# Decode attention over a large KV cache: V in one SBUF buffer and K in two, where K and V shared three in turn

## The chip, the cores and the metric

The kernel runs on one core of one Trainium2 chip. The metric is the device time of one execution in microseconds; shorter is better. Engines are named as the profile names them: PE (TensorE, matrix products; PEld is its weight load), DVE (VectorE), ACT (ScalarE), POOL (GpSimd) and SP (SyncE, which here only issues DMAs).

## What is computed

Two independent blocks A and B, with the same shapes, each compute one decode step of attention. Cut to what matters:

```python
# x (2, 1, 640), k and v (2, 32, 8192, 192), wq (640, 6144), wo (6144, 640), all bfloat16
q = (x @ wq).reshape(B, Sq, H, Dh).transpose(0, 2, 1, 3)
scores = jnp.einsum("bhqd,bhkd->bhqk", q, k_cache) * (Dh ** -0.5)
p = jax.nn.softmax(scores, axis=-1)
o = jnp.einsum("bhqk,bhkd->bhqd", p, v_cache)
y = o.transpose(0, 2, 1, 3).reshape(B, Sq, H * Dh) @ wo
```

The output is the two results side by side. With one query per head, each element of K and V is used once; the two caches of both blocks make up most of the bytes.

## The kernel before, in words

**Units.** The work is cut into 64 units. A unit `u` is two heads of one batch row of one block; its K is 128 partitions x 128 positions x 192 channels (6 MB, 48 KB in each partition), with the two heads in partitions 0-63 and 64-127, and its V has the same form. For a unit:

- `m(u,c)`, c = 0..3: DVE multiplies a quarter of K by the query (`dve_mul`, L285) into one of two product buffers, `prod[c % 2]`.
- `s(u,c)`: PE adds up the product over the channels by 12 matmuls with an identity (`pe_sum`, L362) into a PSUM tile of `scps`; `r(u,c)`: DVE sums the last 16 channels (`dve_red`, L289) into the scores `sc`.
- `mx(u)`: DVE takes the maximum (`dve_max`, L295); `ar(u)`: POOL takes it over the partitions (`pool_ar`, L266); `nb(u)` and `exp(u)`: ACT negates it (L315) and computes the exponentials `pb` and their sums `rs` (`act_exp`, L324).
- `l(u)` and `pv(u)`: PE sums `rs` over the partitions (L368) and multiplies by V in 64 matmuls (`pe_pv`, L376) into `ops`.
- `rc`, `oh`, `os` (DVE, L300 to L306) and `of` (ACT, L309): the division, the result into `qall`.

Before the units, `x` and the two `wq` are loaded and the queries of all heads computed (`pe_q`, L354); after them come a transpose (`pe_turn`, L390) and the product with `wo` (`pe_out`, L404), whose weights are loaded in pieces into buffers that have come free.

**Buffers.** `big` holds three buffers `kv` of a unit's K or V (48 KB of each partition) and the two product buffers. The list `loads` (L209) is k0, k1, v0, k2, v1, ..., k63, v62, v63, and load `i` goes into buffer `i % 3` (L216). All loads are issued by SP in that order on one DMA queue. Load `i` waits for whoever used load `i-3` (`done`, L480): the last product `m(u,3)` for a K, `pv(u)` for a V. The smaller tiles (`sc`, `mp`, `mg`, `nb`, `rs`, `pb`, `rc`, `ops`) and `scps` have three copies each.

**Order of the work.** Each engine's instructions are put into a table by slot and order number (`put`, L418) and emitted in that order; semaphore waits come from the keys. In a slot `u` the order is

- DVE: m(u,0), m(u,1), r(u,0), m(u,2), r(u,1), m(u,3), r(u,2), r(u,3), mx(u), then rc, oh, os of unit u-2;
- PE: s(u,0), s(u,1), s(u,2), s(u,3), l(u-1), pv(u-1);
- ACT: nb(u), exp(u), of(u-2).

DVE, ACT and PE run most units in hardware loops of three units; SP and POOL are straight code.

Of the kernel before, what the change touches and what calls it, by code (L numbers as in the profile page):

```python
# [12 lines left out]
class _Stream:  # L13
    virtual = set()

    def __init__(self, name, sem, reg, first=3):
# [101 lines left out]
def build_kernel(nc, blocks, out):  # L118
# [28 lines left out]
    with ExitStack() as es:  # L147
# [4 lines left out]
        rc = [sb(f"rc{i}", [2, 1], F32) for i in range(3)]  # L152
# [4 lines left out]
        pb = [sb(f"pb{i}", [128, 2 * T], BF16) for i in range(3)]  # L157
        actd = sb("actd", [128, 2], F32)
        xw = sb("xw", [128, NBLK * DC * 128 + D], BF16)
        sc = [sb(f"sc{i}", [128, T], F32) for i in range(3)]  # L160
        mp = [sb(f"mp{i}", [128, 2], F32) for i in range(3)]
        mg = [sb(f"mg{i}", [128, 2], F32) for i in range(3)]
        nb = [sb(f"nb{i}", [128, 1], F32) for i in range(3)]
        rs = [sb(f"rs{i}", [128, 2], F32) for i in range(3)]
# [7 lines left out]
        ops = [ps(f"ops{i}", [128, 512], F32) for i in range(3)]  # L172
        scps = [ps(f"scps{i}", [128, TC, DG], F32) for i in range(3)]
# [3 lines left out]
        oacc = [outps[:], qbank[(LASTU * NCH + 1) % 3]]  # L177
        qps = qbank + [outps[:]]
# [16 lines left out]
        S_pe = _Stream("pe", sem("s_pe"), reg, 1)  # L195
# [16 lines left out]
        loads += [("v", LASTU)]  # L212
        buf = {}
# [6 lines left out]
        bk, b62, b63 = buf["k", LASTU], buf["v", LASTU - 1], buf["v", LASTU]  # L220
        assert (bk, b62, b63) == (2, 0, 1)
        woA, wo0, wo1 = bk * BUFE, b62 * BUFE, b63 * BUFE
        pieces = []
        for blk, rows, off, w in ((0, (WR,), woA, [("s", LASTU, NCH - 1)]), (1, (29,), wo0, [("pv", LASTU - 1)]),
                                  (1, (11, 5, 2, 1), wo1, [("pv", LASTU)])):
            r = 29 if off == wo1 else 0
            for n in rows:
                pieces.append((blk, r, r + n, off, w))
                off, r, w = off + n * D, r + n, []
            assert r == (29 if off == wo0 + 29 * D else WR)  # L230
        NA = 0
        assert 29 * D <= BUFE and woA + WR * D <= NBUF * BUFE + 2 * PRODE
# [21 lines left out]
        def ld_wo(n):  # L254
            blk, r0, r1, off, _ = pieces[n]
            src = blocks[blk]["wo"].rearrange("(p i) n -> p (i n)", i=WR)
            return dma(big[:, off:off + (r1 - r0) * D], src[:, r0 * D:r1 * D], ("wo", n))

        def ld_kv(kind, u):
            hp, b = u // B, u % B  # L260
            blk, h = hp // PPB, 2 * (hp % PPB)
            src = blocks[blk][kind][b, h:h + 2].rearrange("s (p t) d -> (s p) t d", p=64)
            return dma(kv[buf[kind, u]], src, (kind, u))

        def pool_ar(u):
            return lambda eng: eng.partition_all_reduce(mg[u % 3][:], mp[u % 3][:], 128, bass.bass_isa.ReduceOp.max)  # L266
# [21 lines left out]
        def dve_red(u, c):  # L288
            return lambda eng: eng.tensor_reduce(sc[u % 3][:, c * TC:(c + 1) * TC], scps[(u * NCH + c) % 3][:], AXL.X, ALU.add)  # L289

        def dve_max(u):
            def fn(eng):
                for s in range(2):
                    r = slice(64 * s, 64 * s + 64)
                    ins = eng.tensor_reduce(mp[u % 3][r, s:s + 1], sc[u % 3][r, :], AXL.X, ALU.max)  # L295
                return ins
            return fn

        def dve_rc(u):
            return lambda eng: eng.reciprocal(rc[u % 3][:], ops[u % 3][0:2, QW:QW + 1])  # L300

        def dve_ohi(u):
            return lambda eng: eng.tensor_copy(o_hi[:], ops[u % 3][32:34, Dh:QW])  # L303

        def dve_osum(u):
            return lambda eng: eng.tensor_tensor(o_sum[:], ops[u % 3][0:2, 0:Dh], o_hi[:], ALU.add)  # L306

        def act_of(u):
            return lambda eng: eng.activation(qall[0:2, S_act.at(u), :], o_sum[:].unsqueeze(1), ACTF.Identity, scale=rc[u % 3][:])  # L309

        def act_nb(u):
            def fn(eng):
                for s in range(2):
                    r = slice(64 * s, 64 * s + 64)
                    ins = eng.activation(nb[u % 3][r, :], mg[u % 3][r, s:s + 1], ACTF.Identity, scale=-scale)  # L315
# [3 lines left out]
        def act_exp(u):  # L319
            def fn(eng):  # L320
                for s in range(2):
                    r = slice(64 * s, 64 * s + 64)
                    dst = pb[u % 3][r, :].rearrange("p (g a j s) -> p g a j s", a=2, j=JB, s=2)[:, :, :, :, s]
                    ins = eng.activation(dst, sc[u % 3][r, :].rearrange("p (g j a) -> p g a j", j=JB, a=2),  # L324
                                         ACTF.Exp, bias=nb[u % 3][r, :], scale=scale, accum_out=rs[u % 3][r, s:s + 1])
# [33 lines left out]
        def pe_sum(u, c):  # L359
            def fn(eng):  # L360
                for j in range(NJ):
                    ins = eng.matmul(scps[(u * NCH + c) % 3][:], ident[:], prod[c % 2][:, :, j * DG:(j + 1) * DG],  # L362
# [4 lines left out]
        def pe_l(u):  # L367
            return lambda eng: eng.matmul(ops[u % 3][0:2, QW:QW + 1], rs[u % 3][:], ones[:], start=True, stop=True)  # L368

        def pe_pv(u):  # L370
            vv = kv[buf["v", u]].rearrange("p (j a) d -> p j (a d)", a=2)

            def fn(eng):
                for j in range(TJ):
                    j0s = 4 * JB * (j // JB) + 2 * (j % JB)
                    ins = eng.matmul(ops[u % 3][0:MP, 0:QW], pb[u % 3][:, j0s:j0s + MP], vv[:, j, :],  # L376
# [20 lines left out]
        def pe_out(n):  # L397
            blk, r0, r1, off, _ = pieces[n]
            wo = big[:, off:off + (r1 - r0) * D].rearrange("p (i n) -> p i n", n=D)
# [9 lines left out]

        def pe_idle(eng):  # L410
            for i in range(8):
                ins = eng.matmul(ops[(LASTU + 1) % 3][:], ident[:], big[:, woA + 512 * i:woA + 512 * (i + 1)], start=True, stop=True)
            return ins
# [21 lines left out]
        for u in range(NU):  # L435
            for c in range(NCH):
                w = [("k", u), ("pq", NP - 1), ("qa", NP - 1), ("qx", NP - 1), back("s", u, c, 2)]
                slot, order = (0, 9.2) if (u, c) == (1, 0) else (u, 2 + 2 * c)
                put("dve", slot, order, dve_mul(u, c), w, ("m", u, c), ("m", c, u % 3))
                put("dve", u, 5 + 2 * c if c < NCH - 1 else 9.5, dve_red(u, c),  # L440
                    [("s", u, c), key("mx", u - 3), key("exp", u - 3)], ("r", u, c), ("r", c, u % 3))
                put("pe", u, 0.1 * c, pe_sum(u, c),
                    [("m", u, c), ("os", -2) if (u, c) == (1, 0) else None, back("r", u, c, 3), ("id1",), ("qx", NP - 1), ("qa", NP - 1)], ("s", u, c), ("s", c, u % 3))
            put("dve", u, 12, dve_max(u), [("r", u, NCH - 1), key("ar", u - 3), ("init",)], ("mx", u), ("mx", u % 3))
            put("pool", u, 0, pool_ar(u), [("mx", u), key("nb", u - 3)], ("ar", u), ("ar", u % 3))
            put("act", u, 0, act_nb(u), [("ar", u), key("exp", u - 3)], ("nb", u), ("nb", u % 3))
            put("act", u, 1, act_exp(u), [("nb", u), key("pv", u - 3), key("l", u - 3), ("init",)], ("exp", u), ("exp", u % 3))
            w0 = [("exp", u), key("os", u - 3), key("rc", u - 3), ("init",)]
            pslot = u + 1
            pe_o = 2  # L450
            put("pe", pslot, pe_o, pe_l(u), w0, ("l", u), ("l", u % 3))
            put("pe", pslot, pe_o + 0.1, pe_pv(u), [("v", u)], ("pv", u), ("pv", u % 3, buf["v", u]))
            put("dve", u + 2, 20, dve_rc(u), [("pv", u), key("of", u - 3)], ("rc", u), ("rc", u % 3))
            put("dve", u + 2, 21, dve_ohi(u), [("pv", u), key("os", u - 1)], ("oh", u), ("oh", u % 3))
            put("dve", u + 2, 22, dve_osum(u), [("oh", u), key("of", u - 1)], ("os", u), ("os", u % 3))
            put("act", u + 2, 4, act_of(u), [("os", u), ("rc", u)], ("of", u), ("of", u % 3))
# [11 lines left out]
        put("act", NU, 6, act_ot(0), [("t", 1, HQ - 1)], ("ot", 0))  # L468
        put("act", E2, 6, act_ot(1), [("t", 1, HL)], ("ot", 1))
        for n, p in enumerate(pieces):  # L470
# [3 lines left out]
            put("pe", E2, 0.01 * n if n <= NA else 2 + 0.01 * n, pe_out(n), w, ("f", n))  # L474
        put("pe", E2, 1, pe_idle, [("of", LASTU)], None)
# [3 lines left out]

        def done(i):  # L480
            if i < 0:
                return None
            kind, u = loads[i]
            return ("m", u, NCH - 1) if kind == "k" else ("pv", u)
# [10 lines left out]
        for n in range(len(pieces)):  # L495
# [11 lines left out]
        fills = [(mp[i], -3.0e38) for i in range(3)] + [(t[i], 0.0) for i in range(3) for t in (rs, pb)]  # L507
        for n, (t, v) in enumerate(fills):
            S_pool.add((lambda t, v: (lambda eng: eng.memset(t[:], v)))(t, v), sig=("init",) if n == len(fills) - 1 else None)
        for n in range(128 // HP):  # L510
# [10 lines left out]
                              ("r", u, 2), ("r", u, 3), ("mx", u), ("rc", u - 2), ("oh", u - 2), ("os", u - 2)],  # L521
            "act": lambda u: [("nb", u), ("exp", u), ("of", u - 2)],
# [89 lines left out]
```

## Time and profile before

| | |
|---|---|
| median of 3 runs | 1937.36 us (1937.12 to 1937.49) |
| span of the profiled execution | 1936.0 us, 1.4 us under that median (no other time of that execution is given) |
| PE, DVE, ACT, POOL busy | 80%, 58%, 7%, 1% of the span |
| mean granted TensorE clock | 0.929 of full speed |
| moved by DMA | 836.91 MB, mean 432 GB/s |

A share of busy time is an average over the span. The chain of waits follows the work that ended last back from its end. In a timeline row the columns are start and length in us, engine, line, operation, output <- inputs, and in brackets the idle time ahead and who ended it; `SPq` rows are DMA issues. "us to landing" counts from a DMA's issue to its last byte's report.

### The profile page before, as it was taken

The page shows a single profiled execution, that of the slowest core. Times are in us where ns is not written, and L with a number is a line of the kernel's source. Part 1 is how long each engine was busy: PE and PEld are TensorE (multiplying, and loading weights), DVE is VectorE, ACT ScalarE, POOL GpSimd, SP SyncE. Part 2 cuts the span into 40 slices and gives each one's busy share as a digit, 9 for nine tenths or more (in the row PEclk, how much of TensorE's full clock was granted, in tenths as well). Part 3 has the DMA queues.
Part 4 walks back from the last instruction along what each step waited for, and adds up shares of the span by engine and source line. Part 5 has one row for each costly group of instructions (what it writes and reads, how often), then busy time and mean ns, then how long its engine had stood idle before and what let it go on. Part 6 is the DMA issues. An engine that isn't in the chain of part 4 may idle for free.

```text
span 1936.0 us, 19059 instructions
## 1 busy us (share of the span) xinstructions
PE 1545.0 (80%) x7728; PEld 743.0 (38%) x7729; DVE 1124.0 (58%) x907; ACT 142.3 (7%) x519; POOL 28.4 (1%) x113
## 2 busy tenths in 40 slices
PE   5777878878878878878878878878878878878878
PEld 2333434434434434434434434433433433433434
DVE  4765565565565565565565565565565565565560
ACT  3100000000000000000000000000000000000000
POOL 0000000000000000000000000000000000000000
PEclk9899989988989988989988999999999999999999
DMA  9999999999999999999999999999999999999999
GB/s 419 427 435 436 432 434 438 430 434 437 434 433 434 437 431 435 437 432 433 436 436 431 434 438 429 436 437 432 434 435 436 430 436 438 428 436 437 433 433 391
DMA packets 19610, 836.91 MB, mean 432 GB/s; under 512 B 2184, under 2 KB 2320, under 8 KB 2576
## 3 DMA queue, kind: packets, MB, share of 16 engines
q1 hardware_dynamic: 19600, 836.78, 99.9%
q8 instruction: 6, 0.10, 0.0%
q14 instruction: 4, 0.03, 0.0%
HBM read 836.77 MB, written 0.01 MB: 432 GB/s over the span
## 4 chain that ended last, share of the span: by engine, by line
DMA 49%; PE 31%; DVE 17%; issue 3%; DVEq 0%; SPq 0%; ACT 0%; ACTq 0%
DMA big<-in_B_k_cache_dram 24%; DMA big<-in_A_k_cache_dram 22%; PE ops L376 18%; DVE big L285 15%; PE scps L362 12%; DMA big<-in_B_wq_dram 2%; DVE sc L289 1%; DMA big<-in_B_wo_dram 1%; PE scps L354 0%; PE ops L368 0%; PE outps L354 0%; DVEq L285 0%; DVE qall L275 0%; PE scps L404 0%; PE oTps L390 0%
## 5 line engine op out<-in xcount | busy, mean ns | idle before, releaser
L285 DVE TENSOR_TENSOR big<-big,qall 128x6144 bf16<-128x6144 bf16 x256 | 852.7, 3351 | 490.7 <-DMA big<-in_B_k_cache_dram 260.6
L362 PE MATMUL scps<-big,ident 128*128 128x512 bf16 x3072 | 815.6, 426 | 358.2 <-DVE big L285 355.7
L376 PE MATMUL ops<-big,pb 128*34 128x384 bf16 x4096 | 676.8, 326 | 0.0
L362 PEld LDWEIGHTS scps<-big,ident 128*128 128x128 bf16 x3072 | 314.3, 107 | 852.7 <-DVE big L285 439.2
L376 PEld LDWEIGHTS ops<-big,pb 128*34 128x34 bf16 x4096 | 395.5, 98 | 258.7
L289 DVE TENSOR_REDUCE sc<-scps 128x32 f32<-128x512 f32 x256 | 175.9, 687 | 227.7 <-PE scps L362 227.7
L315 ACT ACTIVATE nb<-mg 64x1 f32<-64x1 f32 x128 | 25.8, 201 | 1707.7 <-POOL mg L266 1706.9
L324 ACT ACTIVATE pb<-sc,nb 64x128 bf16<-64x128 f32 x128 | 55.8, 436 | 7.8
L266 POOL PARTITION_ALL_REDUCE mg<-mp x64 | 25.7, 402 | 1859.1 <-DVE mp L295 1859.1
L295 DVE TENSOR_REDUCE mp<-sc 64x1 f32<-64x128 f32 x128 | 35.9, 280 | 8.3
L309 ACT ACTIVATE qall<-o_sum,rc 2x192 f32 (+1 forms) x64 | 29.0, 453 | 20.7 <-DVE o_sum L306 19.1
L306 DVE TENSOR_TENSOR o_sum<-ops,o_hi 2x192 f32<-2x192 f32 x64 | 22.1, 346 | 7.7
L354 PE MATMUL scps<-big,xw 128*128 x120 | 23.2, 351 | 2.6 <-DVE xw L271 2.2
L324 ACT ACTIVATION_READ_ACCUMULATOR pb<-sc,nb 64x1 f32 x128 | 23.7, 185 | 0.0
L303 DVE COPY o_hi<-ops 2x192 f32<-2x192 f32 x64 | 22.3, 349 | 2.0
L300 DVE RECIPROCAL rc<-ops 2x1 f32<-2x1 f32 x64 | 10.0, 156 | 21.3 <-PE ops L376 19.3
L275 DVE CAST qall<-scps 64x192 f32 x48 | 17.0, 355 | 7.2 <-PE scps L354 5.4
L280 ACT ACTIVATE qall<-scps 64x192 f32 x48 | 15.6, 324 | 30.5 <-DVE qall L275 28.2
L345 PE MATMUL oTps<-ident,xw 4*128 4x4 bf16 x5 | 0.4, 178 | 21.5 <-DMA xw<-in_B_x_dram 21.5
L354 PEld LDWEIGHTS scps<-big,xw 128*128 128x128 bf16 x120 | 12.4, 103 | 12.1 <-issue 5.9
L368 PEld LDWEIGHTS ops<-ones,rs 128*2 128x2 f32 x128 | 5.5, 82 | 26.9 <-issue 26.9
L404 PE MATMUL outps<-big,oT 128*2 128x320 bf16 x96 | 9.2, 369 | 4.6 <-DMA big<-in_A_wo_dram 4.6
(36 smaller groups left out, 67.6 us busy)
## 6 DMA issues: line engine op xcount, KB each, us to landing
big<-in_A_k_cache_dram SPq DMA_DIRECT2D x32, 6144.0 KB, 28.6
big<-in_A_v_cache_dram SPq DMA_DIRECT2D x32, 6144.0 KB, 27.6
big<-in_B_k_cache_dram SPq DMA_DIRECT2D x32, 6144.0 KB, 28.9
big<-in_B_v_cache_dram SPq DMA_DIRECT2D x32, 6144.0 KB, 27.8
big<-in_A_wq_dram SPq DMA_DIRECT2D x1, 7680.0 KB, 21.2
big<-in_B_wq_dram SPq DMA_DIRECT2D x1, 7680.0 KB, 38.2
big<-in_A_wo_dram SPq DMA_DIRECT2D x1, 7680.0 KB, 29.0
big<-in_B_wo_dram SPq DMA_DIRECT2D x1, 4640.0 KB, 29.3
```

The source lines that it names most:

```text
L266: return lambda eng: eng.partition_all_reduce(mg[u % 3][:], mp[u % 3][:], 128, bass.bass_isa.ReduceOp.max)
L285: return lambda eng: eng.tensor_tensor(prod[c % 2], t[:, c * TC:(c + 1) * TC, :], qall[:, S_dve.at(u), :].broadcast_to([128, TC, Dh]), ALU ...
L289: return lambda eng: eng.tensor_reduce(sc[u % 3][:, c * TC:(c + 1) * TC], scps[(u * NCH + c) % 3][:], AXL.X, ALU.add)
L295: ins = eng.tensor_reduce(mp[u % 3][r, s:s + 1], sc[u % 3][r, :], AXL.X, ALU.max)
L303: return lambda eng: eng.tensor_copy(o_hi[:], ops[u % 3][32:34, Dh:QW])
L306: return lambda eng: eng.tensor_tensor(o_sum[:], ops[u % 3][0:2, 0:Dh], o_hi[:], ALU.add)
L309: return lambda eng: eng.activation(qall[0:2, S_act.at(u), :], o_sum[:].unsqueeze(1), ACTF.Identity, scale=rc[u % 3][:])
L315: ins = eng.activation(nb[u % 3][r, :], mg[u % 3][r, s:s + 1], ACTF.Identity, scale=-scale)
L324: ins = eng.activation(dst, sc[u % 3][r, :].rearrange("p (g j a) -> p g a j", j=JB, a=2), ACTF.Exp, bias=nb[u % 3][r, :], scale=scale, acc ...
L354: ins = eng.matmul(qps[hp % NQ][:, 0:QW], xbc[:, blk, c, :], wq_t[blk][:, c, S_pe.at(off, QW, QW)], start=(c == 0), stop=(c == DC - 1))
L362: ins = eng.matmul(scps[(u * NCH + c) % 3][:], ident[:], prod[c % 2][:, :, j * DG:(j + 1) * DG], start=(j == 0), stop=(j == NJ - 1))
L376: ins = eng.matmul(ops[u % 3][0:MP, 0:QW], pb[u % 3][:, j0s:j0s + MP], vv[:, j, :], start=(j == 0), stop=(j == TJ - 1))
```

## The change

- **Buffers.** V always has buffer 2; K of unit u has buffer `u % 2`. So the load of k(u) waits for m(u-2,3), and that of v(u) for pv(u-1). The order of the loads on SP stays, up to the last ones.
- **Order on PE:** s(u,0), s(u,1), s(u,2), l(u-1), pv(u-1), s(u,3): the V product stands ahead of the fourth quarter's sums.
- **Order on DVE:** m(u,1), r(u,0), m(u,2), r(u,1), m(u,3), r(u,2), rc, oh, os of u-1, then m(u+1,0) of the next unit, then r(u,3), mx(u).
- **Order on ACT:** of(u-1), nb(u), exp(u).
- **Tiles.** The small tiles have one copy each instead of three, `scps` has four copies (one a quarter), the query phase uses these four.
- **Loops** of one unit on PE and ACT, of two on DVE and (new) on SP; POOL stays straight code.
- **Tail.** 38 of the 48 rows of A's `wo` (rows of 128 x 640) are loaded into K's buffer 0 after m(62,3), ahead of v(63); 10 rows of A and 28 of B follow into the K buffers after s(63,3), 19 rows of B into the product buffers and one into `xw`. No piece of `wo` waits for pv(63) now. The 8 matmuls of `pe_idle` (L410) are gone, and A's first 38 rows are multiplied ahead of pv(63).

```diff
-        for i, (kind, u) in enumerate(loads):
-            buf[kind, u] = i % NBUF
-            bcount[i % NBUF] += 1
-            reg[(kind, u)] = (bsem[i % NBUF], 16 * bcount[i % NBUF])
+            n = VB if kind == "v" else u % VB
+            buf[kind, u] = n
+            bcount[n] += 1
+            reg[(kind, u)] = (bsem[n], 16 * bcount[n])
...
-                slot, order = (0, 9.2) if (u, c) == (1, 0) else (u, 2 + 2 * c)
-                put("dve", slot, order, dve_mul(u, c), w, ("m", u, c), ("m", c, u % 3))
+                put("dve", u if c else u - 1, 2 + 2 * c if c else 9.3, dve_mul(u, c), w, ("m", u, c), ("m", c, u % VB))
                 put("dve", u, 5 + 2 * c if c < NCH - 1 else 9.5, dve_red(u, c),
-                    [("s", u, c), key("mx", u - 3), key("exp", u - 3)], ("r", u, c), ("r", c, u % 3))
-                put("pe", u, 0.1 * c, pe_sum(u, c),
+                    [("s", u, c), key("exp", u - 1)], ("r", u, c), ("r", c))
+                put("pe", u, 0.1 * c if c < NCH - 1 else 3, pe_sum(u, c),
...
-            put("dve", u + 2, 20, dve_rc(u), [("pv", u), key("of", u - 3)], ("rc", u), ("rc", u % 3))
+            put("dve", u + 1, 9.20, dve_rc(u), [("pv", u), key("of", u - 1)], ("rc", u), ("rc",))
...
-        for i, (kind, u) in enumerate(loads):
-            w = [done(i - NBUF)]
-            if i in (1, 2):
-                w = [("pq", PPB * i - 1)]
-            S_sp.add(ld_kv(kind, u), waits=w)
+        for kind, u in loads[:-1]:
+            if kind == "k":
+                load(kind, u, [("pq", PPB - 1)] if u == 1 else [key("m", u - VB, NCH - 1)] if u else [])
+            else:
+                load(kind, u, [key("pv", u - 1)] if u else [("pq", NP - 1)])
+        S_sp.add(ld_wo(0), waits=pieces[0][4])
+        load("v", LASTU, [("pv", LASTU - 1)])
+        for n in range(1, len(pieces)):
             S_sp.add(ld_wo(n), waits=pieces[n][4])
...
-                S_dve.emit(eng, [(PQ0, PQ0 + NP, NQ), (3, NSLOT, 3)])
+                S_dve.emit(eng, [(PQ0, PQ0 + NP, NQ), (1, NSLOT, VB)])
...
-                S_pe.emit(eng, [(PQ0, PQ0 + PPB, NQ), (PQ0 + PPB, PQ0 + NP, NQ), (1, NSLOT, 3)])
+                S_pe.emit(eng, [(PQ0, PQ0 + PPB, NQ), (PQ0 + PPB, PQ0 + NP, NQ), (1, NSLOT, 1)])
```

`VB` is 2, `NCH` 4, `LASTU` 63.

More of the change, by code (lines that the diff above doesn't have):

```diff
@@ L14, with __init__ @@
     virtual = set()
-    def __init__(self, name, sem, reg, first=3):
+    def __init__(self, name, sem, reg, first=1):
         self.first = first
@@ L150, in build_kernel @@
         sem = lambda name: es.enter_context(nc.semaphore(name))
-        rc = [sb(f"rc{i}", [2, 1], F32) for i in range(3)]
+        rc = sb("rc", [2, 1], F32)
+        nb = sb("nb", [128, 1], F32)
+        rs = sb("rs", [128, 2], F32)
         o_hi = sb("o_hi", [2, Dh], F32)
@@ L156, in build_kernel @@
         qall = sb("qall", [128, NU, Dh], BF16)
-        pb = [sb(f"pb{i}", [128, 2 * T], BF16) for i in range(3)]
+        pb = sb("pb", [128, 2 * T], BF16)
         actd = sb("actd", [128, 2], F32)
         xw = sb("xw", [128, NBLK * DC * 128 + D], BF16)
[L160 to L164, printed above, removed]
+        sc = sb("sc", [128, T], F32)
+        mp = sb("mp", [128, 2], F32)
+        mg = sb("mg", [128, 2], F32)
         ident = sb("ident", [128, 128], BF16)
@@ L170, in build_kernel @@
         out_sb = sb("out_sb", [HP + B, D], BF16)
-        ops = [ps(f"ops{i}", [128, 512], F32) for i in range(3)]
-        scps = [ps(f"scps{i}", [128, TC, DG], F32) for i in range(3)]
+        ops = ps("ops", [128, 512], F32)
+        scps = [ps(f"scps{i}", [128, TC, DG], F32) for i in range(NCH)]
         outps = ps("outps", [128, 512], F32)
@@ L215, in build_kernel @@
         for i, (kind, u) in enumerate(loads):
-            buf[kind, u] = i % NBUF
-            bcount[i % NBUF] += 1
-            reg[(kind, u)] = (bsem[i % NBUF], 16 * bcount[i % NBUF])
-        bk, b62, b63 = buf["k", LASTU], buf["v", LASTU - 1], buf["v", LASTU]
-        assert (bk, b62, b63) == (2, 0, 1)
-        woA, wo0, wo1 = bk * BUFE, b62 * BUFE, b63 * BUFE
+            n = VB if kind == "v" else u % VB
+            buf[kind, u] = n
+            bcount[n] += 1
+            reg[(kind, u)] = (bsem[n], 16 * bcount[n])
+        FREE0, FREE1 = [("m", LASTU - 1, NCH - 1)], [("m", LASTU, NCH - 1), ("s", LASTU, NCH - 1)]
+        BIG, XW = 0, 1
+        PROD = NBUF * BUFE
         pieces = []
-        for blk, rows, off, w in ((0, (WR,), woA, [("s", LASTU, NCH - 1)]), (1, (29,), wo0, [("pv", LASTU - 1)]),
-                                  (1, (11, 5, 2, 1), wo1, [("pv", LASTU)])):
-            r = 29 if off == wo1 else 0
+        for blk, rows, t, off, w in ((0, (38, 10), BIG, 0, FREE0), (1, (28,), BIG, WR * D, FREE1),
+                                     (1, (12, 5, 2), BIG, PROD, []), (1, (1,), XW, 0, [])):
             for n in rows:
[L228 to L232, printed above, removed]
+                r = sum(p[2] - p[1] for p in pieces if p[0] == blk)
+                pieces.append((blk, r, r + n, (t, off), w))
+                off, w = off + n * D, FREE1 if t == BIG and off == 0 else []
+        assert sum(p[2] - p[1] for p in pieces) == NBLK * WR
+        assert 76 * D <= VB * BUFE and 19 * D <= 2 * PRODE
+        NA = 1
         for n in range(len(pieces)):
@@ L288, in dve_red @@
         def dve_red(u, c):
-            return lambda eng: eng.tensor_reduce(sc[u % 3][:, c * TC:(c + 1) * TC], scps[(u * NCH + c) % 3][:], AXL.X, ALU.add)
+            return lambda eng: eng.tensor_reduce(sc[:, c * TC:(c + 1) * TC], scps[c][:], AXL.X, ALU.add)
         def dve_max(u):
@@ L299, in dve_rc @@
         def dve_rc(u):
-            return lambda eng: eng.reciprocal(rc[u % 3][:], ops[u % 3][0:2, QW:QW + 1])
+            return lambda eng: eng.reciprocal(rc[:], ops[0:2, QW:QW + 1])
         def dve_ohi(u):
-            return lambda eng: eng.tensor_copy(o_hi[:], ops[u % 3][32:34, Dh:QW])
+            return lambda eng: eng.tensor_copy(o_hi[:], ops[32:34, Dh:QW])
         def dve_osum(u):
-            return lambda eng: eng.tensor_tensor(o_sum[:], ops[u % 3][0:2, 0:Dh], o_hi[:], ALU.add)
+            return lambda eng: eng.tensor_tensor(o_sum[:], ops[0:2, 0:Dh], o_hi[:], ALU.add)
         def act_of(u):
-            return lambda eng: eng.activation(qall[0:2, S_act.at(u), :], o_sum[:].unsqueeze(1), ACTF.Identity, scale=rc[u % 3][:])
+            return lambda eng: eng.activation(qall[0:2, S_act.at(u), :], o_sum[:].unsqueeze(1), ACTF.Identity, scale=rc[:])
         def act_nb(u):
@@ L361, in fn @@
                 for j in range(NJ):
-                    ins = eng.matmul(scps[(u * NCH + c) % 3][:], ident[:], prod[c % 2][:, :, j * DG:(j + 1) * DG],
+                    ins = eng.matmul(scps[c][:], ident[:], prod[c % 2][:, :, j * DG:(j + 1) * DG],
                                      start=(j == 0), stop=(j == NJ - 1))
@@ L367, in pe_l @@
         def pe_l(u):
-            return lambda eng: eng.matmul(ops[u % 3][0:2, QW:QW + 1], rs[u % 3][:], ones[:], start=True, stop=True)
+            return lambda eng: eng.matmul(ops[0:2, QW:QW + 1], rs[:], ones[:], start=True, stop=True)
         def pe_pv(u):
@@ L375, in fn @@
                     j0s = 4 * JB * (j // JB) + 2 * (j % JB)
[L376 removed]
+                    ins = eng.matmul(ops[0:MP, 0:QW], pb[:, j0s:j0s + MP], vv[:, j, :],
                                      start=(j == 0), stop=(j == TJ - 1))
@@ L397, in pe_out @@
         def pe_out(n):
-            blk, r0, r1, off, _ = pieces[n]
-            wo = big[:, off:off + (r1 - r0) * D].rearrange("p (i n) -> p i n", n=D)
+            blk, r0, r1, (t, off), _ = pieces[n]
+            wo = (big, xw)[t][:, off:off + (r1 - r0) * D].rearrange("p (i n) -> p i n", n=D)
             def fn(eng):
@@ L408, in pe_out @@
             return fn
[L410 to L413, printed above, removed]
         NSLOT = NU + 8
@@ L447, in build_kernel @@
-            put("act", u, 1, act_exp(u), [("nb", u), key("pv", u - 3), key("l", u - 3), ("init",)], ("exp", u), ("exp", u % 3))
-            w0 = [("exp", u), key("os", u - 3), key("rc", u - 3), ("init",)]
+                    [("s", u, c), key("exp", u - 1)], ("r", u, c), ("r", c))
+                put("pe", u, 0.1 * c if c < NCH - 1 else 3, pe_sum(u, c),
+                    [("m", u, c), back("r", u, c, NCH), ("id1",), ("qx", NP - 1), ("qa", NP - 1)], ("s", u, c), ("s", c))
+            put("dve", u, 12, dve_max(u), [("r", u, NCH - 1), key("ar", u - 1), ("init",)], ("mx", u), ("mx",))
@@ L489, in build_kernel, with load @@
         S_sp.add(ld_wq(1))
-        for i, (kind, u) in enumerate(loads):
-            w = [done(i - NBUF)]
-            if i in (1, 2):
-                w = [("pq", PPB * i - 1)]
-            S_sp.add(ld_kv(kind, u), waits=w)
-        for n in range(len(pieces)):
+        def load(kind, u, w):
+            slot = u if kind == "k" else u + 1
+            blk = u // UPB
+            S_sp.add(ld_kv(kind, u), waits=w, tag=(slot, (kind, u % B, blk)))
+        for kind, u in loads[:-1]:
[6 more added lines that the diff above has]
+        for n in range(1, len(pieces)):
             S_sp.add(ld_wo(n), waits=pieces[n][4])
@@ L506, in build_kernel @@
         S_pool.add(lambda eng: eng.memset(ones[:], 1.0))
-        fills = [(mp[i], -3.0e38) for i in range(3)] + [(t[i], 0.0) for i in range(3) for t in (rs, pb)]
+        fills = [(mp, -3.0e38), (rs, 0.0), (pb, 0.0)]
         for n, (t, v) in enumerate(fills):
@@ L520, in build_kernel @@
             "dve": lambda u: [("m", u, 0), ("m", u, 1), ("r", u, 0), ("m", u, 2), ("r", u, 1), ("m", u, 3),
-                              ("r", u, 2), ("r", u, 3), ("mx", u), ("rc", u - 2), ("oh", u - 2), ("os", u - 2)],
-            "act": lambda u: [("nb", u), ("exp", u), ("of", u - 2)],
-            "pe": lambda u: [("s", u, c) for c in range(NCH)] + [("l", u - 1), ("pv", u - 1)],
+                              ("r", u, 2), ("rc", u - 1), ("oh", u - 1), ("os", u - 1), ("r", u, 3), ("mx", u)],
+            "act": lambda u: [("of", u - 1), ("nb", u), ("exp", u)],
+            "pe": lambda u: [("s", u, 0), ("s", u, 1), ("s", u, 2), ("l", u - 1), ("pv", u - 1), ("s", u, 3)],
             "pool": lambda u: [("ar", u)],
@@ L527, in build_kernel @@
         for name, keys in per_unit.items():
-            pre[keys(0)[0]] = [k for u in (-3, -2, -1) for k in keys(u)]
-            for u in range(3):
-                late = [k for k in keys(u) if k[1] < 0]
-                if late:
-                    post[[k for k in keys(u) if k[1] >= 0][-1]] = late
+            real = [k for k in keys(0) if k[1] >= 0][0]
+            pre[real] = [k for u in (-3, -2, -1) for k in keys(u)]
+            for k in keys(0):
+                if k[1] >= 0:
+                    real = k
+                else:
+                    (pre if real == [k for k in keys(0) if k[1] >= 0][0] else post).setdefault(real, []).append(k)
         for name, S in (("dve", S_dve), ("act", S_act), ("pe", S_pe), ("pool", S_pool)):
```

60 lines of the change are left out of this document (28 added, 32 removed).

## The prediction

> **What bounds the kernel now.** I read the page first: engine shares, the DMA row, the chain. The queue row gives packet time as a share of 16 engines' span.
>
> ```profile
> span 1936.0 us, 19059 instructions
> DMA  9999999999999999999999999999999999999999
> q1 hardware_dynamic: 19600, 836.78, 99.9%
> HBM read 836.77 MB, written 0.01 MB: 432 GB/s over the span
> DMA 49%; PE 31%; DVE 17%; issue 3%; DVEq 0%; SPq 0%; ACT 0%; ACTq 0%
> L285 DVE TENSOR_TENSOR big<-big,qall 128x6144 bf16<-128x6144 bf16 x256 | 852.7, 3351 | 490.7 <-DMA big<-in_B_k_cache_dram 260.6
> ```
>
> The DMA engines are busy 99.9% of the span, while DVE waits 490.7 us for K. The chain names PE and DVE for half of the time, but only because it follows each load back to whoever let it be *issued*; the load then stood in the queue behind another. So the bytes set the time. The change moves no bytes: it can gain next to nothing, and it loses whenever the queue runs empty. The question is therefore when each load is issued against when the queue would be through with the one ahead. For that I read two units from the timeline, and the loads in the chain:
>
> ```profile
> 1016.50 0.19 PE L368 MATMUL ops<-ones,rs 128*2 128x1 f32 x2
> 1016.62 10.57 PE L376 MATMUL ops<-big,pb 128*34 128x384 bf16 x64
> 1017.42 0.57 DVE L295 TENSOR_REDUCE mp<-sc 64x1 f32<-64x128 f32 x2
> 1018.03 0.16 DVE L300 RECIPROCAL rc<-ops 2x1 f32<-2x1 f32 x1
> 1018.69 0.35 DVE L306 TENSOR_TENSOR o_sum<-ops,o_hi 2x192 f32<-2x192 f32 x1
> 1027.01 6.63 DVE L285 TENSOR_TENSOR big<-big,qall 128x6144 bf16<-128x6144 bf16 x2 [7.97 <-DMA big<-in_B_k_cache_dram]
> 1030.42 8.32 PE L362 MATMUL scps<-big,ident 128*128 128x512 bf16 x24 [3.22 <-DVE big L285]
> 1035.76 0.69 DVE L289 TENSOR_REDUCE sc<-scps 128x32 f32<-128x512 f32 x1 [2.13 <-PE scps L362]
> 1036.37 3.35 DVE L285 TENSOR_TENSOR big<-big,qall 128x6144 bf16<-128x6144 bf16 x1
> 1039.78 2.76 PE L362 MATMUL scps<-big,ident 128*128 128x512 bf16 x12 [1.03 <-DVE big L285]
> 1043.64 2.76 PE L362 MATMUL scps<-big,ident 128*128 128x512 bf16 x12 [1.10 <-DVE big L285]
> 1046.34 0.19 PE L368 MATMUL ops<-ones,rs 128*2 128x1 f32 x2
> 1046.46 10.57 PE L376 MATMUL ops<-big,pb 128*34 128x384 bf16 x64
> 1056.01 6.63 DVE L285 TENSOR_TENSOR big<-big,qall 128x6144 bf16<-128x6144 bf16 x2 [7.14 <-DMA big<-in_B_k_cache_dram]
> 1057.06 0.33 SPq L245 DMA_DIRECT2D big<-in_B_k_cache_dram  x1
> 1059.43 7.04 PE L362 MATMUL scps<-big,ident 128*128 128x512 bf16 x24 [2.40 <-DVE big L285]
> 1063.90 0.69 DVE L289 TENSOR_REDUCE sc<-scps 128x32 f32<-128x512 f32 x1 [1.26 <-PE scps L362]
> 1027.23 28.63 DMA big<-in_B_k_cache_dram
> ```
>
> K lands every 1056.01 - 1027.01 = 29.0 us, two loads of 14.5 us. The load issued at 1027.23 lands at 1055.86, 28.6 us later: it waited half of that. This is the cover that the change spends. DVE starts 0.15 us after the landing, and SP issues 0.03 us after the V product that frees the buffer (1046.46 + 10.57 = 1057.03).
>
> **The change part by part.** *V's single buffer, steady state.* Count from K(u)'s landing. With the queue full, V(u-1) lands at 14.5 and K(u+1) at 29.0; v(u) must then follow at once, and it waits for pv(u-1). That product now stands behind s(u,2) only. Its chain: m(u,0) starts at 0.15 and s(u,0) 3.41 later (1027.01 to 1030.42), at 3.56. PE's first matmuls after its idle time run slowly, so r(u,0) comes 5.34 (1030.42 to 1035.76) or 4.47 (1059.43 to 1063.90) after that: at 8.9 or 8.0. On DVE r(u-1,3), mx(u-1) and m(u,1) now stand between: 0.15 + 3.3 + 0.8 + 0.6 + 3.3 = 8.1, so 8.1 is the lower value. The old exp(u-1) must also be done (`sc` has one copy); from mx to the end of exp it takes about 2 us, so by 6.8: hidden. Then m(u,2) 0.61 later, s(u,2) 3.41 after it, l and pv 2.81 later (1043.64 to 1046.46): pv(u-1) starts at 14.9 or 15.7, just after V's landing, and ends 10.57 later at 25.5 or 26.3. The issue is at 25.6 or 26.4, with 0.05 more for the registers of SP's new loop, which I take from nothing shown (bounds 0 and 0.3; a loop on the other engines shows no idle of its own between units). k(u+2) waits behind it on SP; its own condition m(u,3) is met by about 16.5, and it has 14.5 us to spare.
>
> So v(u) is issued 2.6 to 3.4 us before the queue runs empty, where the old loads had 14. Whether this is enough depends on what an issue needs before its bytes flow. The trace has one load on an empty queue:
>
> ```profile
> 0.72 0.40 SPq L245 DMA_DIRECT2D big<-in_A_wq_dram  x1
> big<-in_A_wq_dram SPq DMA_DIRECT2D x1, 7680.0 KB, 21.2
> GB/s 0 0 983 328 0 82 819 410 82 819 410 82 819 410 82 819 410 82 819 410 0 901 410 0 819 492 0 826 492 0 819 492 0 819 492 0 819 492 0 655
> 1925.08 9.93 SPq L245 DMA_DIRECT2D out_dram<-out_sb  x2
> ```
>
> At 14.5 us for 6144 KB, 7680 KB are 18.1 us; the landing took 21.2, so 3.1 us were dead. The third row (slices of 0.75 us of the first 30) shows packets starting in the third slice, 0.8 to 1.5 us after the issue; the rest of the 3.1 is slow first packets and the report. Bounds for the need: 0.8 us below, 3.1 above. With 3.1 the long chain is late by 26.4 + 3.1 - 29.0 = 0.5 us and the short one not at all; with 1.5 none is. How often is the chain long? In this trace both lengths alternate; I take one unit in four, as the clock's phase drifts (mean granted clock 0.92 in 115 to 1000 us, 0.94 in 1000 to 1850):
>
> ```profile
> 115.00:1000.00 885.00, 722.72 (x3492) 344.36 (x3490) 518.56 (x397) 57.41 (x217) 10.97 (x31) 0.92 1.00 434
> 1000.00:1850.00 850.00, 676.74 (x3330) 324.87 (x3330) 505.37 (x381) 53.70 (x203) 10.27 (x29) 0.94 1.00 434
> 1850.00:1936.00 86.00, 69.80 (x537) 36.85 (x538) 27.03 (x31) 5.96 (x20) 0.71 (x2) 0.94 0.95 409
> ```
>
> 16 units by 0.5 us are 8 us, by nothing 0. A queue still busy with the load ahead should hide part of the slow start, so I take **half, +3.7 us** (0 to 8).
>
> The Trainium skill, page "Trainium Kernel Development and Optimization", section "Best Practices", says to double-buffer so that DMA and compute overlap. V's single buffer goes against that; read strictly, the queue would stand still for each product, 10.57 us by 62 units, some 655 us. No row here shows a single buffer; the K loads between the V loads are why I don't follow it.
>
> *The start.* Here the queue does run empty. v1 waited for m(1,3) and went at 89.39; now it waits for pv(0).
>
> ```profile
> 77.18 3.42 POOL L266 PARTITION_ALL_REDUCE mg<-mp  x1 [73.94 <-DVE mp L295]
> 81.59 0.44 ACT L324 ACTIVATE pb<-sc,nb 64x128 bf16<-64x128 f32 x1
> 81.54 0.69 DVE L289 TENSOR_REDUCE sc<-scps 128x32 f32<-128x512 f32 x1 [1.16 <-PE scps L362]
> 85.56 2.76 PE L362 MATMUL scps<-big,ident 128*128 128x512 bf16 x12 [1.46 <-DVE big L285]
> 98.96 3.36 DVE L285 TENSOR_TENSOR big<-big,qall 128x6144 bf16<-128x6144 bf16 x1 [5.43 <-DMA big<-in_A_k_cache_dram]
> 102.84 25.30 DMA big<-in_A_k_cache_dram
> ```
>
> POOL's first reduction takes 3.42 us, so exp(0) ends at 82.1 (81.59 + 0.44 and a read). r(1,0), at 81.54 before, now needs it: 0.6 us later. s(1,2) goes from 85.56 to 86.15, pv(0) starts 2.81 later at 88.96 and ends at 99.53; v1 is issued at 99.57. K2 landed at 98.9, so nothing is left in the queue. Then v1 and k3 behind it land 99.57 + 3.1 + 29.0 = 131.7; k3 landed at 102.84 + 25.30 = 128.14. **The hole costs 3.5 us** (1.9 if an issue needs only 1.5). Nothing later has slack to repay it.
>
> *Edits at nothing.* rc, oh, os of u-1 now stand ahead of m(u+1,0); pv ends at 26.3 at the latest and they take 1.0 us (1018.03 to 1018.69 + 0.35), so at 27.3, before K(u+1) at 29.0: hidden by the wait for K, and beyond 1.7 us more they would delay every unit. s(u,3) ends at 26.3 + 2.8 = 29.1, needed by r(u,3) at 32.4. The single copies of `ops`, `pb`, `nb`, `mg` are free by then. Query phase: four banks as before, ahead of K. The loops' branches fall into idle time of PE and ACT; DVE's falls every second unit between mx and m, 0.1 to 0.2 us where r(u,0) has up to 0.8 to spare.
>
> *The tail.* Same bytes, all issued before the queue needs them: wo's first 38 rows behind v62, v63 after pv(62) with one load of cover, the rest after s(63,3), 14 us before v63 has landed. DMA share in 1850 to 1936 is 0.95 already; the last piece is again one row. 0, with 1 us either way.
>
> **Sum.** On the span 1936.0 + 3.5 + 3.7 = 1943.2; with the 1.4 us by which the median stands above it, **1944.6 us**.
>
> **The rivals.**
> *A: the queue is late in every unit.* If PE starts cold in the long way each time (its idle stays some 3.5 us, and 3.22 was enough above) and the need is 3.1, each v is late by 0.46. As K(u+2) hangs on K(u), two units share it: 0.23 by 62 = 14.3. 1937.4 + 3.5 + 14.3 = 1955. For: both rows are from this trace. Against: half of the units here had the short start.
> *B: an issue needs little.* Need 1.5: no bubble, hole 1.9, 1939.3, within the bound of no change. For: packets flow 0.8 to 1.5 us after the issue. Against: 21.2 us of landing.
> The Trainium skill, "DMA: Bandwidth & Descriptors", section "Anatomy of one DMA — SWDGE (gpsimd) path", puts a DMA's fixed part at about 2.0 us, most of it at the end; by that the hole would be 2.4, no steady bubble, 1939.8 (an estimate). The first load's 3.1 us speaks against it, at least for a cold start.
> *C: not slower.* The tail repays the hole. Of the last 86 us, 5% (4.3 us) are without packets; some 2 us are the output's way out (issue at about 1934.7, end 1936.0) and the last sums. If the new order fills the other 2.2 us and the hole is 1.9, the time is 1937.1. It decides once hole and bubbles stay under 2.2. Against: one last small piece and the output's path are as before.
> *D: the loop on SP does not do what it is meant to*, each issue costing 1 us or more for registers and addresses: 0.5 to 0.6 by 62 on top of A, 1965 to 1995. Against: a loop on PE, ACT and DVE shows nothing of this size.
>
> **How the numbers follow.** Forecast 45% (1941 to 1949), A 25% (1949 to 1965), B 20% (1939 to 1941), C 3%, D 7%. The range **1939 to 1962** leaves out D, C and the top of A, some 15 to 18%. This kernel's measurement tells 0.2% (3.9 us: 1933.5 and 1941.2) from no change. Slower: forecast, A, D less the lowest edge, 0.74; same: B, C and that edge, 0.25; faster 0.01, for no case reaches it.
>
> **What would show it.** In the changed profile: v1 issued near 99.6 and k3 landing near 131.7; pv starts 15 to 15.7 us after K's landing and v issued near 26; K every 29.0 to 29.2 us (A: 29.2 to 29.3; B: 29.0; D: 29.5 or more), DMA share 1.00 to 0.99. I am wrong if pv starts later than 16 us after K, if DVE is late for m(u+1,0), or if the hole at 99 is missing.

## The result, and the profile after

The changed kernel takes **2042.1 us** (median of 5 runs, 2038.0 to 2046.0) against 1937.4 before: a ratio of 1.054, 95% interval 1.0527 to 1.0553. The direction was forecast; 1944.6 and the range up to 1962 were far too low.

First the page of the changed kernel, the rows that answer to those of before:

```profile
span 2037.3 us, 19807 instructions
q1 hardware_dynamic: 19744, 836.78, 96.9%
HBM read 836.77 MB, written 0.01 MB: 411 GB/s over the span
DMA 50%; PE 25%; DVE 8%; issue 8%; POOL 6%; ACT 2%; SPq 1%; DVEq 0%; ACTq 0%; POOLq 0%
L288 DVE TENSOR_TENSOR big<-big,qall 128x6144 bf16<-128x6144 bf16 x256 | 858.0, 3352 | 85.2 <-DMA big<-in_A_k_cache_dram 45.7
L269 POOL PARTITION_ALL_REDUCE mg<-mp x64 | 221.5, 3461 | 1775.1 <-DVE mp L298 1775.1
L303 DVE RECIPROCAL rc<-ops 2x1 f32<-2x1 f32 x64 | 9.9, 155 | 631.4 <-PE ops L379 631.4
big<-in_B_v_cache_dram SPq DMA_DIRECT2D x32, 6144.0 KB, 17.2
```

The bytes are the same, the queue is busy 96.9% in place of 99.9%, and DVE hardly waits for K any more (85 us where it was 491) but with `rc` for the V product (631 us). A load of B's V lands 17.2 us after its issue (A's 18.2), where 14.5 us are its own bytes: it found the queue empty or nearly so. And POOL, easily passed over with 11% of the span, stands in the chain with 6%. Its row before was this:

```profile
L266 POOL PARTITION_ALL_REDUCE mg<-mp x64 | 25.7, 402 | 1859.1 <-DVE mp L295 1859.1
```

The same 64 reductions took 0.40 us on average and now take 3.46. One unit of the changed kernel's timeline (K had landed at 1021.9; rows in between are left out) shows why, and whom it reaches:

```profile
1022.02 3.36 DVE L288 TENSOR_TENSOR big<-big,qall 128x6144 bf16<-128x6144 bf16 x1 [1.41 <-DMA big<-in_B_k_cache_dram]
1026.10 0.57 DVE L298 TENSOR_REDUCE mp<-sc 64x1 f32<-64x128 f32 x2
1026.70 3.36 DVE L288 TENSOR_TENSOR big<-big,qall 128x6144 bf16<-128x6144 bf16 x1
1026.77 3.51 POOL L269 PARTITION_ALL_REDUCE mg<-mp  x1 [26.19 <-DVE mp L298]
1030.39 0.41 ACT L318 ACTIVATE nb<-mg 64x1 f32<-64x1 f32 x2 [9.20 <-POOL mg L269]
1031.96 0.69 DVE L292 TENSOR_REDUCE sc<-scps 128x32 f32<-128x512 f32 x1 [1.90 <-ACT pb L327]
1032.57 3.35 DVE L288 TENSOR_TENSOR big<-big,qall 128x6144 bf16<-128x6144 bf16 x1
1035.97 5.30 PE L365 MATMUL scps<-big,ident 128*128 128x512 bf16 x12 [3.09 <-DVE big L288]
1041.33 10.84 PE L379 MATMUL ops<-big,pb 128*34 128x384 bf16 x64
1052.20 0.33 SPq L265 DMA_DIRECT2D big<-in_B_v_cache_dram  x1
```

The reduction starts 0.07 us after m(u,1) and ends 0.2 us after it (1030.28 against 1030.06): it stands still while DVE multiplies. In all 63 units where the two overlap it ends 0.21 to 0.22 us after the multiplication. The order of before put only DVE's short rc and oh, which read `ops` in PSUM, behind mx, and beside them the reduction was short:

```profile
1018.09 0.35 POOL L266 PARTITION_ALL_REDUCE mg<-mp  x1 [27.83 <-DVE mp L295]
```

The new order puts a multiplication right behind mx. From there the delay runs on: nb at 1030.39, exp, and then r(u,0) at 1031.96, 10.1 us after K's landing, because `sc` has one copy now. PE, idle for 3.09 us ahead of s(u,2), starts slowly again (5.30 us for 12 matmuls against 2.76). The V product starts 19.4 us after the landing (18.0 on average over the units), v is issued at 1052.20, and K(u+1) landed at 1052.4: nothing is left in the queue.

### The profile page after: what moved, and what is told of

It is laid out like the page before. It is cut to its first block, busy times and chain, and to the rows that moved or that the text cites. A ratio compares the mean times of both kernels' runs of the same rounds, so it can differ in the third digit from the quotient of the medians.

```text
span 2037.3 us, 19807 instructions
## 1 busy us (share of the span) xinstructions
PE 1568.3 (77%) x7721; PEld 742.7 (36%) x7721; DVE 1125.3 (55%) x907; ACT 142.1 (7%) x519; POOL 223.6 (11%) x107
## 3 DMA queue, kind: packets, MB, share of 16 engines
q1 hardware_dynamic: 19744, 836.78, 96.9%
## 4 chain that ended last, share of the span: by engine, by line
DMA 50%; PE 25%; DVE 8%; issue 8%; POOL 6%; ACT 2%; SPq 1%; DVEq 0%; ACTq 0%; POOLq 0%
DMA big<-in_B_k_cache_dram 25%; DMA big<-in_A_k_cache_dram 22%; PE ops L379 17%; PE scps L365 7%; DVE big L288 6%; POOL mg L269 6%; DMA big<-in_B_wo_dram 2%; DVE sc L292 1%; PE scps L357 1%; ACT pb L327 1%; DMA xw<-in_B_x_dram 1%; DMA big<-in_B_v_cache_dram 1%; SPq L265 1%; DVE mp L298 1%; ACT nb L318 0%
## 5 line engine op out<-in xcount | busy, mean ns | idle before, releaser
L365 PE MATMUL scps<-big,ident 128*128 128x512 bf16 x3072 | 841.6, 434 | 433.1 <-DVE big L288 433.1
L269 POOL PARTITION_ALL_REDUCE mg<-mp x64 | 221.5, 3461 | 1775.1 <-DVE mp L298 1775.1
L312 ACT ACTIVATE qall<-o_sum,rc 2x192 f32 x64 | 29.0, 454 | 1253.4 <-DVE o_sum L309 1253.4
L357 PE MATMUL scps<-big,xw 128*128 x160 | 28.5, 342 | 3.3 <-DVE xw L274 2.2
L278 DVE CAST qall<-scps 64x192 f32 x64 | 22.7, 355 | 8.2 <-PE scps L357 5.6
L283 ACT ACTIVATE qall<-scps 64x192 f32 x64 | 20.7, 324 | 32.2 <-DVE qall L278 29.8
## 6 DMA issues: line engine op xcount, KB each, us to landing
big<-in_A_v_cache_dram SPq DMA_DIRECT2D x32, 6144.0 KB, 18.2
big<-in_B_v_cache_dram SPq DMA_DIRECT2D x32, 6144.0 KB, 17.2
```

The lines of the kernel that those rows point to most:

```text
L269: return lambda eng: eng.partition_all_reduce(mg[:], mp[:], 128, bass.bass_isa.ReduceOp.max)
L278: return lambda eng: eng.tensor_copy(qall[ro, S_dve.at(B * hp + 1 - s, 1, B), :], qps[hp % NQ][ri, s * Dh:(s + 1) * Dh].unsqueeze(1))
L357: ins = eng.matmul(qps[hp % NQ][:, 0:QW], xbc[:, blk, c, :], wq_t[blk][:, c, S_pe.at(off, QW, QW)], start=(c == 0), stop=(c == DC - 1))
L365: ins = eng.matmul(scps[c][:], ident[:], prod[c % 2][:, :, j * DG:(j + 1) * DG], start=(j == 0), stop=(j == NJ - 1))
```

## The experiments

Two theories at the outset: **P**, POOL's reduction held up by DVE's multiplication, reaching the V product through exp and the one copy of `sc`; and **H**, the handover of V's single buffer, which costs the time whatever POOL does. Medians, each against runs of before on the same chip:

| kernel | us | ratio to before, 95% |
|---|---|---|
| changed | 2042.1 | 1.0527 to 1.0553 |
| + m(u,1) waits for POOL | 2000.2 | 1.0314 to 1.0349 |
| two copies of `sc` | 1997.7 | 1.0291 to 1.0325 |
| ring of three buffers kept | 1945.7 | 1.0033 to 1.0067 |
| SP straight code | 2046.1 | 1.0540 to 1.0575 |
| old order of the fourth quarter | 2063.9 | 1.0631 to 1.0664 |
| V handed back in halves | 1944.8 | 1.0025 to 1.0056 |
| halves + wait for POOL | 1940.7 | 1.0010 to 1.0028 |
| parted at 48 of 64 + wait | 1941.6 | 1.0012 to 1.0031 |
| parted at 56 of 64 + wait | 1948.9 | 1.0047 to 1.0100 |

**A wait more.**

```diff
                 w = [("k", u), ("pq", NP - 1), ("qa", NP - 1), ("qx", NP - 1), back("s", u, c, 2)]
+                if c == 1:
+                    w.append(key("ar", u - 1))
```

> Only edit to the changed kernel: m(u,1) on DVE also waits for ar(u-1), POOL's reduction. Theory P (POOL's reduction stands still while DVE multiplies, and r(u,0) waits for it through exp(u-1) and the one copy of sc): the reduction falls from 3.46 us to about 0.35, r(u,0) comes 8.6 to 8.9 us after K's landing instead of 10.1, the V product starts 15.4 to 15.7 after it in place of 17 to 19.5, and the time falls from 2042 to between 1955 and 1985 (what is left is the late issue of v). Rival H (the handover of V's single buffer costs the time by itself, whatever POOL does): the reduction gets short but the time stays above 2025.

Adding a wait takes 42 us away. The queue's and the reduction's rows on that kernel's page, and the same stretch of its timeline:

```profile
q1 hardware_dynamic: 19744, 836.78, 98.9%
L269 POOL PARTITION_ALL_REDUCE mg<-mp x64 | 22.7, 354 | 1934.6 <-DVE mp L298 1934.6
```

```profile
1029.96 3.36 DVE L288 TENSOR_TENSOR big<-big,qall 128x6144 bf16<-128x6144 bf16 x1 [3.30 <-DMA big<-in_B_k_cache_dram]
1034.62 0.35 POOL L269 PARTITION_ALL_REDUCE mg<-mp  x1 [29.86 <-DVE mp L298]
1035.13 3.36 DVE L288 TENSOR_TENSOR big<-big,qall 128x6144 bf16<-128x6144 bf16 x1 [0.60 <-POOL mg L269]
1038.40 0.68 DVE L292 TENSOR_REDUCE sc<-scps 128x32 f32<-128x512 f32 x1
1045.23 10.57 PE L379 MATMUL ops<-big,pb 128*34 128x384 bf16 x64
1055.98 0.34 SPq L265 DMA_DIRECT2D big<-in_B_v_cache_dram  x1
1059.44 3.36 DVE L288 TENSOR_TENSOR big<-big,qall 128x6144 bf16<-128x6144 bf16 x1 [2.69 <-DMA big<-in_B_k_cache_dram]
```

DVE pays 0.60 us here, the reduction is 0.35 us every time, the first one too, and the V product starts 15.4 us after the landing, as in the chain that the prediction had worked out. P holds. But 2000 lies above P's 1955 to 1985 and below H's 2025, so both theories have a share, and v, issued 3.3 us before K lands, still comes too late: units take 30.0 us.

**Two copies of `sc`.** `sc` is indexed by `u % 2` (so ACT's loop has two units), and r(u,0) waits for another exp:

```diff
-                    [("s", u, c), key("exp", u - 1)], ("r", u, c), ("r", c))
+                    [("s", u, c), key("exp", u - 2)], ("r", u, c), ("r", c, u % 2))
```

> Only edit to the changed kernel: the scores sc have two copies, so r(u,0) waits for exp(u-2) and not exp(u-1). Theory P: POOL's reduction stays at 3.46 us but nobody on the way to the V product waits for it; r(u,0) at 8.1 to 8.9 after K's landing, time 1950 to 1985, within 10 us of the kernel with the added wait. Rival H: above 2025. Rival Q (the long reduction hurts by itself, wherever sc stands): no gain, above 2030.

1997.7 us, with the reduction still at its full length:

```profile
L269 POOL PARTITION_ALL_REDUCE mg<-mp x64 | 221.6, 3462 | 1733.4 <-DVE mp L298 1733.4
```

So the long reduction by itself costs nothing that can be seen here; it costs where someone on the way to the V product waits for it. Rival Q falls. The level is that of the kernel with the added wait, 13 us above the upper end expected.

**The ring of three kept.** The buffers, the waits of the loads and the tail are those of before, SP is straight code again and PE's loop has three units; the new order of the engines and the single small tiles stay.

```diff
-            n = VB if kind == "v" else u % VB
-            buf[kind, u] = n
+            buf[kind, u] = i % NBUF
...
-        for kind, u in loads[:-1]:
+        for i, (kind, u) in enumerate(loads):
+            w = [done(i - NBUF)]
```

> The changed kernel with the buffers, the loads' waits and the tail of the kernel before (three buffers in turn, SP straight code), and all else of the change: order on PE, DVE and ACT, single small tiles, loops of one unit on ACT. Theory P with H's buffers as its condition: POOL's reduction still takes about 3.4 us and r(u,0) still comes late, but the loads are issued a whole load ahead, so the time is 1937 to 1943. Rival O (the new order of the engines, not the buffers, costs the time): above 2000.

1945.7: the new order with its long reductions (3461 ns on its page too) costs nothing when loads are issued some 9 us ahead; in the trace's landing records no load after k(1) is late. The 8 us are in the tail, which was put back with the buffers but not with the order: A's `wo` waits for s(63,3), now behind pv(62).

```profile
1900.96 0.33 SPq L245 DMA_DIRECT2D big<-in_A_wo_dram  x1
```

Before, it was issued at 1886.20; v(63) landed at 1896.7 in that run, so here the queue stood empty. Its landing comes 7.8 us later (1923.0 against 1915.2). The expectation missed by this.

**SP straight code.** `S_sp.emit(eng)` without the loops.

> Only edit to the changed kernel: SP's loads as straight code instead of loops of two units. Theory P: an issue comes 0.03 us after the V product in place of 0.03 to 0.18, time 2030 to 2042. Rival D of the prediction (SP's loop costs about 1 us an issue): the time falls below 2000.

2046.1: no gain, and 4 us above the range expected. SP's loop is not the cause; rival D of the prediction falls.

**The old order of the fourth quarter.**

```diff
-                put("pe", u, 0.1 * c if c < NCH - 1 else 3, pe_sum(u, c),
+                put("pe", u, 0.1 * c, pe_sum(u, c),
...
-            put("dve", u, 12, dve_max(u), [("r", u, NCH - 1), key("ar", u - 1), ("init",)], ("mx", u), ("mx",))
+            put("dve", u, 9.15, dve_max(u), [("r", u, NCH - 1), key("ar", u - 1), ("init",)], ("mx", u), ("mx",))
```

(and r(u,3) from 9.5 to 9.1).

> The changed kernel with the old order around the fourth quarter: s(u,3) ahead of the V product on PE, r(u,3) and mx(u) ahead of rc, oh, os on DVE. The reduction then runs while DVE waits for the V product, so 0.35 us. Theory: the V product starts 19.5 us after K's landing and ends at 30, DVE waits for it with rc before it can begin the next K, so a unit takes about 31.1 us: 2060 to 2080, slower than the changed kernel although its reduction is short. Rival (the long reduction is what the new order costs, and the old order is as good): 2000 or less.

2063.9, as expected, with reductions of 0.35 us (all but the first):

```profile
1025.36 10.58 PE L379 MATMUL ops<-big,pb 128*34 128x384 bf16 x64
1026.82 0.35 POOL L269 PARTITION_ALL_REDUCE mg<-mp  x1 [30.38 <-DVE mp L298]
1035.96 0.34 SPq L265 DMA_DIRECT2D big<-in_A_v_cache_dram  x1
1037.99 6.63 DVE L288 TENSOR_TENSOR big<-big,qall 128x6144 bf16<-128x6144 bf16 x2 [1.11 <-DMA big<-in_B_k_cache_dram]
```

With these buffers, moving the V product ahead gains 22 us net: it brings the issue forward by more than the reduction it slows down costs.

**V handed back in halves.** Theory **L** for the rest: with one buffer v can be issued at most 29.0 - 14.5 - 10.6 = 3.9 us before the queue runs empty. Two parts of the V product and two loads of V break that bound:

```diff
-            put("pe", pslot, pe_o + 0.1, pe_pv(u), [("v", u)], ("pv", u), ("pv",))
+            put("pe", pslot, pe_o + 0.1, pe_pv(u, 0), [("va", u)], ("pva", u), ("pva",))
+            put("pe", pslot, pe_o + 0.2, pe_pv(u, 1), [("v", u)], ("pv", u), ("pv",))
...
-                load(kind, u, [key("pv", u - 1)] if u else [("pq", NP - 1)])
+                load("va", u, [key("pva", u - 1)] if u else [("pq", NP - 1)])
+                load("v", u, [key("pv", u - 1)] if u else [])
```

> The changed kernel with V's buffer handed back in halves and nothing else: POOL's reduction stays at 3.46 us. Theory L: the V product still starts 17 to 19.5 us after K's landing, so its first half is issued 3.4 to 7 us before the queue runs empty; most of the 105 us go, time 1940 to 1965. Rival P alone (without the added wait the long reduction keeps its price of about 42 us): above 1975.

> The kernel with the added wait for ar(u-1), and V's buffer handed back in halves: the V product in two parts of 32 matmuls, V loaded by two DMAs of 3072 KB, the first waiting for the first part of the product before. Theory L (what is left of the loss is only the short lead of v's issue: one buffer gives at most 29.0 - 14.5 - 10.6 = 3.9 us, and the engines lose 0.3 to 2 us a load below some 4.5): the first half is issued about 8 us before the queue runs empty, no load lands late, time 1937 to 1943. Rival S (two buffers' worth of bytes in flight are not enough, or single small tiles cost): above 1960.

1944.8 without and 1940.7 with the wait for POOL. On the first one's page the reduction is as long as ever and the queue is full:

```profile
q1 hardware_dynamic: 28960, 836.79, 100.0%
L273 POOL PARTITION_ALL_REDUCE mg<-mp x64 | 221.5, 3461 | 1682.5 <-DVE mp L302 1682.5
```

Theory L holds, and "P alone" falls: POOL's 42 us are paid only where v's issue has no time to spare. So the two causes are not two prices to be added freely: the short lead is the condition, the reduction makes it shorter.

**Parted later.** The same, parted after 48 and after 56 matmuls instead of 32.

> The kernel with the added wait and V's buffer handed back in two parts, but parted after 48 of the 64 matmuls: the first part of v is issued about 23.6 us after K's landing, 5.4 us before the last engine and some 3.5 us before the first engine is through with the load ahead. Theory T (a load must be issued 3.0 us before the FIRST of the 16 engines runs dry; later than that, the last engine's landing slips as well): still no load late, 1939 to 1946. Rival (what helped was the small loads or the two parts as such, in proportion to how early they come): 1950 or more.

> The same, parted after 56 of 64 matmuls: issued about 24.9 us after K's landing, 4.1 us before the last engine and 2.2 to 2.6 us before the first one is through. Theory T: the first engines run dry, 0.3 to 0.6 us are lost a unit, 1955 to 1980. Rival of the prediction's sum (3.1 us before the LAST engine's landing are enough): no load late, 1939 to 1946.

At 48, 1941.6, as theory T has it. At 56 the runs lie between 1942.7 and 1959.2 (median 1948.9), below theory T's 1955 and above the rival's 1946: neither. The profiled run (1943.4) is one of the fastest of them; there the first parts of V were late by 3.3 us in all. The trace tells each of the 16 engines' reports, so the lead of v's issue, the time from it to the end of the load ahead, can be counted against the first and the last engine to finish that load, and the lateness against 14.5 us a load. Where V comes in two parts, both are those of the first part, against its share of the 14.5 us; the whole of V is then 0.04 to 0.08 us late:

| kernel | lead on the first engine, us | on the last | last landing late, mean of 62 (old order: 61, without v1) |
|---|---|---|---|
| old order of the fourth quarter | 0.03 | 1.11 | 1.87 |
| changed | 0.72 | 1.85 | 1.58 |
| + wait for POOL | 1.25 | 3.46 | 0.89 |
| two copies of `sc` | 1.34 | 3.50 | 0.87 |
| parted at 56 | 3.08 | 4.11 | 0.05 |
| halves, no wait | 3.15 | 4.76 | 0.05 |
| parted at 48 | 3.16 | 5.42 | 0.03 |
| halves + wait | 6.09 | 7.99 | 0.02 |

Some 3 us on the first engine, some 4 on the last, is where the loss ends. Whether the first or the last one sets it isn't settled, as no pair of these kernels parts the two clearly; at the edge, runs of one kernel differ by 16 us.

## Why the prediction was wrong

By its own steps:

- *The bytes set the time; the change can only lose where the queue runs empty:* right as to the place. The landings of V are late by 98 us in sum (62 by 1.58), nearly all of the 101 us between the spans. But an empty queue is only part of it: the packets took 96.9% of 2037.3 us, 1974 us, in place of 99.9% of 1936.0, 1934 us. So some 40 of the 101 us are packets of the same bytes that took longer, and 61 are idle engines. With the added wait it is 42 of 62 (98.9% of 1998.0). In the trace the longer packets stand around the handover from K to V.
- *"The old exp(u-1) must also be done (...) from mx to the end of exp it takes about 2 us, so by 6.8: hidden":* **this step failed**, and 42 of the 105 us hang on it with these buffers. From the end of mx to the end of exp it takes 5.2 us on average (1026.67 to 1031.93 in the unit shown), where it was 2.0 before. The 2 us hold where no multiplication runs beside the reduction, as at 1018.09 before. The row that contradicts it stood in the prediction's own fence: 77.18 with 3.42 us, taken for "POOL's first reduction". It ran beside m(1,1), and it was the only one of the 64 that ran beside a multiplication. With the added wait the first one too takes 0.35. This is the timeline of before at that place:

```profile
77.03 3.36 DVE L285 TENSOR_TENSOR big<-big,qall 128x6144 bf16<-128x6144 bf16 x1
```

- *The rest of the chain, pv at 14.9 to 15.7:* right where the step above is mended: 15.4 in the timeline shown, 15.8 on average. In the changed kernel it is 18.0 on average, later than the 16 us that the prediction named as a sign of being wrong; PE's second slow start, at s(u,2), came with it, as the wait for exp lengthened its idle time to 3.09 us. The sign was not enough: with the mended chain it is not met, and 62 us of span are lost all the same.
- *The steady lateness, "half, +3.7 us (0 to 8)":* **the mis-sized term.** In the kernel with the mended chain it is 55 us (62 by 0.89; 2.6 of them are the hole at the start). Three choices made it small, and what each weighs isn't shown: the need of 3.1 us was counted against the last engine's landing, while the engines finish 1 to 2 us apart; a busy queue was trusted to hide half of the need, and at a mean lead of 3.5 the loads were 0.89 late all the same; and the chain was taken as long in one unit of four only. The bound of 8 was therefore no bound.
- *The hole at the start, 3.5 us:* right in place and nearly in size: v1 was issued at 100.7 (predicted 99.57), k3 landed at 132.9 (131.7), 4.8 us later than before. This hole is part of the 98 us above.
- *SP's loop at 0.05 us, the edits at nothing, the tail at 0:* right; straight code gains nothing, and the span ends 2.1 us after the last landing (2037.3 and 2035.2), as before (1936.0 and 1933.9). rc did become DVE's great wait (631 us), but it is the V product's lateness seen from DVE.
- *The rivals:* A had the right place (late in every unit) with a seventh of the price, D the nearest price with the wrong cause. None had POOL.
- *The double-buffer rule,* cited and set aside: its strict price (655 us) is far off, yet its direction was right: the time came as a short lead, not as a standstill for each product.

The Trainium skill, page "SBUF — State Buffer", section "Who interferes with whom", states the rule that was missed: a DVE instruction with two SBUF inputs and a GpSimd instruction that reads SBUF block each other, and the second to be issued waits. The traces agree: the multiplication reads `big` and `qall`, the reduction behind it takes 3.51 us in place of 0.354. That it is a port, no run here shows.

What stays open: the 3.4 us that the best variant (1940.7) keeps over the kernel before. Its two loads take 29.04 us a unit in place of 29.00, which would be 2.5 us, but whether that is the smaller pieces of V wasn't tried. No version here beats the kernel before; its queue is 99.9% busy.

## What to carry to other kernels

A buffer's handover is judged by its lead: how long before the queue runs empty the next load is issued, against some 4 us here, and not by whether its wait "ends in time". When an order is changed, look for what each engine's instruction will now run beside, small ones off the path too: one odd duration among 64 equal ones is a finding, not a first call. Where a buffer can't be doubled, hand it back in parts.

## What the runs showed of the hardware that was not expected

- POOL's reduction over the partitions takes 0.354 us without a DVE multiplication beside it and 3.51 with one of 3.36; adding a wait on DVE made the kernel 42 us faster.
- Beside DVE's short copies from PSUM the same reduction keeps its 0.354 us: it is not any work on DVE that holds it up.
- A load issued on an empty queue lands about 3 us after what its bytes take (17.4 to 17.7 us for 14.5, the four such loads of V in the changed kernel); one issued 3.5 us before the queue is through still lands 0.9 us late on average.
- A busy queue is not proof of full speed: with the added wait it is 98.9% busy, and two thirds of the 62 us lost are packets that took longer.
